# Storing the last output piece by two DMAs from two queues

## The chip, the cores and the metric

The kernel runs on one core of a Trainium2 chip. The metric is the device time of one execution in microseconds; medians of repeated runs are quoted, with the lowest and highest. *Span* is the time from the first to the last instruction in the profile; it is listed for every run, to 0.1 us, so that a single difference of time and span is good to 0.05 us. *Tail* is the part of the span after the end of the last VectorE addition, read from the profiled run. Times finer than the printed lines (1617.775 where a line has 1617.78), first packets of single DMAs and landings come from the records of the same trace.

## The reference

Four blocks with residual connections on x of 2048 tokens by 1024 columns, in bf16: linear attention, gated feed-forward, and the same two again. Only the end of the last block matters here:

```python
def _B_ref(x, w_gate, w_up, w_down):
    g = jnp.einsum("bsd,df->bsf", x, w_gate)
    u = jnp.einsum("bsd,df->bsf", x, w_up)
    h = g * u
    return jnp.einsum("bsf,fd->bsd", h, w_down)
...
x = x + _B_ref(_layernorm(x, axis=-1), B_w_gate, B_w_up, B_w_down)
return x
```

## The kernel before

X holds all tokens in 16 tiles of 128 tokens. In the last block each tile's sum is added to X by VectorE and stored at once by SyncE. The last tile is done in three column pieces of 512, 384 and 128 columns, so that little is left to add and store after the last matmul:

```python
def add_store(t, a, b, ps, last):
    nc.vector.tensor_tensor(out=X[:, t, a:b], in0=X[:, t, a:b], in1=ps, op=ALU.add)
    if last:
        nc.sync.dma_start(out=o_view[:, t, a:b], in_=X[:, t, a:b])
...
def d_end(t):
    def run():
        tl = t % TPG
        for a, b in ((0, 512), (512, 896), (896, 1024)):
            ps = mm_tile()
            for f in range(KF):
                nc.tensor.matmul(out=ps[:, 0, 0:b - a], lhsT=hT[:, f, tl * P:(tl + 1) * P], rhs=wd[f][:, a:b],
                                 start=(f == 0), stop=(f == KF - 1))
            add_store(t, a, b, ps[:, 0, 0:b - a], True)
    return run
```

All DMAs of the program are issued by SyncE. At the end SyncE waits for the semaphores of all of them, two in each wait instruction, and then all engines meet in a barrier.

## Time and profile before

| | before |
|---|---|
| time, 3 runs | 1622.09 us (1621.53 to 1622.28) |
| span of the profiled run | 1620.06 us |
| TensorE busy | 1607.5 us |
| last VectorE addition ends | 1617.75 us |
| last store: start, first packet, last packet, landing | 1617.78, 1618.60, 1618.88, 1619.23 us |
| tail | 2.31 us |

The change can act only on the last row, the tail. The lines behind the table stand in the prediction.

### The profile page before, as it was taken

To read this page: it belongs to the slowest core of one execution; us is meant where nothing else is said; L and a number is where in the kernel's file an instruction comes from. 1 tells how busy PE (TensorE), PEld (TensorE's weight loads), DVE (VectorE), ACT (ScalarE), POOL (GpSimd) and SP (SyncE) were. 2 spreads that over 40 slices of the span, in tenths; PEclk is the share of its full clock that TensorE was granted. 3 is DMA by queue.
4 is the path that set the end of the run, shared out by engine and by line. 5 is a ranking of instruction groups with operands and counts; after the bars stand their busy time and mean duration, and the time that the engine had idled before them with its cause. 6 is when DMAs were issued, how large, how long until landed. Compare 5 with 4: busy or idle time off the path is not lost.

```text
span 1620.1 us, 18047 instructions
## 1 busy us (share of the span) xinstructions
PE 1607.5 (99%) x7710; PEld 734.5 (45%) x7861; DVE 616.6 (38%) x946; ACT 284.0 (18%) x384; POOL 54.5 (3%) x135
## 2 busy tenths in 40 slices
PE   9999999999999999999999999999999999999999
PEld 4444444444444444444444444444444444444444
DVE  6899853202311321243255798432123113211111
ACT  5522201101110110011045231011011101101110
POOL 2100000000000000010000000000000000000000
DMA  8224856512650552142420257655236306521400
GB/s 247 53 72 93 246 162 176 162 52 60 171 159 0 147 162 81 52 156 66 92 52 1 78 114 219 181 157 165 69 102 175 127 20 173 165 66 65 156 1 26
DMA packets 236719, 183.10 MB, mean 113 GB/s; under 512 B 102368, under 2 KB 217312, under 8 KB 236640
## 3 DMA queue, kind: packets, MB, share of 16 engines
q1 hardware_dynamic: 236640, 181.95, 39.0%
q8 instruction: 61, 1.00, 0.3%
q14 instruction: 18, 0.15, 0.0%
HBM read 153.09 MB, written 4.19 MB: 97 GB/s over the span
## 4 chain that ended last, share of the span: by engine, by line
PE 99%; issue 1%; DMA 0%; SPq 0%; DVE 0%
PE ps L196 50%; PE ps L538 48%; PE ps L565 1%; DMA W<-in_A_wqkv_dram 0%; PE kv L306 0%; SPq L109 0%; PE pm L328 0%; PE ps L328 0%; DVE X L546 0%
## 5 line engine op out<-in xcount | busy, mean ns | idle before, releaser
L538 PE MATMUL ps<-xT,R 128*128 128x512 bf16 x2382 | 525.9, 379 | 2.6
L538 PEld LDWEIGHTS <-R 128*128 128x128 bf16 x2432 | 238.0, 98 | 286.9
L542 DVE TENSOR_TENSOR R<-gs,ps 128x512 bf16<-128x512 f32 x224 | 153.9, 687 | 533.5 <-ACT gs L541 533.5
L196 PEld LDWEIGHTS <-R 128*128 128x128 bf16 x2248 | 220.0, 98 | 265.2
L541 ACT COPY gs<-ps 128x512 f32<-128x512 f32 x224 | 131.3, 586 | 1040.2 <-PE ps L538 1011.5
L538 PE MATMUL ps<-xT,W 128*128 128x512 bf16 x1130 | 250.4, 379 | 1.2
L196 PEld LDWEIGHTS <-xT 128*128 128x128 bf16 x1536 | 149.5, 98 | 181.4 <-issue 1.9
L196 PE MATMUL ps<-W,xT 128*128 128x512 bf16 x997 | 222.8, 379 | 1.9 <-issue 0.3
L538 PEld LDWEIGHTS <-W 128*128 128x128 bf16 x1152 | 112.7, 98 | 135.9
L196 PE MATMUL ps<-W,R 128*128 128x512 bf16 x733 | 170.1, 379 | 0.8
L546 DVE TENSOR_TENSOR X<-X,ps 128x1024 bf16<-128x1024 bf16 (+3 forms) x34 | 39.4, 1158 | 335.8 <-PE ps L196 282.8
L196 PE MATMUL ps<-R,R 128*128 128x512 bf16 x506 | 111.8, 379 | 0.4
L196 PE MATMUL ps<-PQ,R 128*128 128x512 bf16 x488 | 111.4, 379 | 0.5
L196 PE MATMUL ps<-R,xT 128*128 128x512 bf16 x502 | 110.3, 379 | 0.5
L201 ACT ACTIVATE e<-ps 128x1024 bf16<-128x1024 f32 x56 | 57.3, 1024 | 141.2 <-PE ps L196 86.0
L175 DVE BATCH_NORM_STATS2 st<-X 128x6 f32<-128x512 bf16 x128 | 81.7, 680 | 0.1
L179 POOL TENSOR_SCALAR ve<-mv 128x1 f32<-128x1 f32 x64 | 16.2, 254 | 1325.8 <-DVE mv L177 1325.8
L196 PE MATMUL ps<-GL,R 128*128 128x512 bf16 x240 | 57.8, 379 | 0.3
L196 PE MATMUL ps<-xT,R 128*128 128x512 bf16 x240 | 57.5, 379 | 0.2
L378 DVE TENSOR_TENSOR X<-X,ps 128x1024 bf16<-128x1024 bf16 x32 | 38.7, 1209 | 17.0 <-PE ps L196 17.0
L186 DVE TENSOR_SCALAR R<-X,mv,rstd 128x1024 bf16<-128x1024 bf16 x64 | 33.7, 542 | 27.3 <-POOL rstd L181 24.0
L205 DVE TENSOR_SCALAR e<-e 128x1024 bf16<-128x1024 bf16 x64 | 26.9, 421 | 38.1 <-ACT e L201 38.1
(73 smaller groups left out, 456.6 us busy)
## 6 DMA issues: line engine op xcount, KB each, us to landing
R<-in_B_w_gate_dram SPq DMA_DIRECT2D x38, 1024.0 KB, 5.4
R<-in_B_w_up_dram SPq DMA_DIRECT2D x38, 1024.0 KB, 7.6
W<-in_B_w_gate_dram SPq DMA_DIRECT2D x18, 1024.0 KB, 5.4
W<-in_B_w_up_dram SPq DMA_DIRECT2D x18, 1024.0 KB, 7.6
W<-in_A_wqkv_dram SPq DMA_DIRECT2D x10, 1024.0 KB, 6.2
W<-in_B_w_down_dram SPq DMA_DIRECT2D x6, 1024.0 KB, 11.2
X<-in_A_x_dram SPq DMA_DIRECT2D x16, 256.0 KB, 6.7
PQ<-in_B_w_down_dram SPq DMA_DIRECT2D x4, 1024.0 KB, 8.4
```

The costliest lines, as they stand in the source:

```text
L175: nc.vector.bn_stats(out=st[:, c, :], in_=X[:, t, c * NB:(c + 1) * NB])
L179: nc.gpsimd.tensor_scalar(out=ve[:], in0=mv[:, 1:2], scalar1=1e-5, scalar2=None, op0=ALU.add)
L186: nc.vector.tensor_scalar(out=dst, in0=X[:, t, :], scalar1=mv[:, 0:1], scalar2=rstd[:], op0=ALU.subtract, op1=ALU.mult)
L196: nc.tensor.matmul(out=ps[:, n, :], lhsT=lhsT, rhs=rhs[:, n * NB:(n + 1) * NB], start=start, stop=stop)
L201: nc.scalar.activation(out=e[:], in_=flat(ps), func=ACT.Exp, **sc)
L205: nc.vector.tensor_scalar(out=e[:], in0=e[:], scalar1=1.0, scalar2=EPS, op0=ALU.min, op1=ALU.add)
L378: nc.vector.tensor_tensor(out=X[:, t, :], in0=X[:, t, :], in1=flat(ps), op=ALU.add)
L538: nc.tensor.matmul(out=ps[:, n, :], lhsT=w[:, k, j * P:(j + 1) * P], rhs=xT[g % 2][:, k, :], start=(k == 0), stop=(k == KD - 1))
L541: nc.scalar.copy(out=gs[:], in_=ps[:, 0, :])
L542: nc.vector.tensor_tensor(out=hT[:, f, :], in0=gs[:], in1=ps[:, 1, :], op=ALU.mult)
L546: nc.vector.tensor_tensor(out=X[:, t, a:b], in0=X[:, t, a:b], in1=ps, op=ALU.add)
L565: nc.tensor.matmul(out=ps[:, 0, 0:b - a], lhsT=hT[:, f, tl * P:(tl + 1) * P], rhs=wd[f][:, a:b], start=(f == 0), stop=(f == KF - 1))
```

## The change

The intent is to shorten the tail: two queues issue half of the last piece each, so that each DMA has half of the tokens to move.

```diff
-                add_store(t, a, b, ps[:, 0, 0:b - a], True)
+                nc.vector.tensor_tensor(out=X[:, t, a:b], in0=X[:, t, a:b], in1=ps[:, 0, 0:b - a], op=ALU.add)
+                if b < D:
+                    nc.sync.dma_start(out=o_view[:, t, a:b], in_=X[:, t, a:b])
+                else:
+                    for eng, h in ((nc.sync, 0), (nc.scalar, 64)):
+                        eng.dma_start(out=o_view[h:h + 64, t, a:b], in_=X[h:h + 64, t, a:b])
```

## The prediction

> **What bounds the kernel now.** I read the page first, its engine shares and the chain of work that ended last.
>
> ```profile
> PE 1607.5 (99%) x7710; PEld 734.5 (45%) x7861; DVE 616.6 (38%) x946; ACT 284.0 (18%) x384; POOL 54.5 (3%) x135
> ...
> PE 99%; issue 1%; DMA 0%; SPq 0%; DVE 0%
> PE ps L196 50%; PE ps L538 48%; PE ps L565 1%; DMA W<-in_A_wqkv_dram 0%; PE kv L306 0%; SPq L109 0%; PE pm L328 0%; PE ps L328 0%; DVE X L546 0%
> ```
>
> TensorE is busy for 1607.5 of 1620.1 us and the chain is 99% matmuls. The change touches no matmul. It can act only on what follows the last matmul, so I went to the end of the span: the chain and the timeline of the last microseconds.
>
> ```profile
> 1609.85 7.58 PE ps L565 x62
> 1617.44 0.02 issue
> 1617.46 0.29 DVE X L546
> ...
> 1616.48 1.63 SPq L548 DMA_DIRECT2D out_dram<-X  x2
> ...
> 1617.46 0.29 DVE L546 TENSOR_TENSOR X<-X,ps 128x128 bf16<-128x128 bf16 x1 [1.01 <-PE ps L565]
> ```
>
> The columns are start, duration, what. The last matmul group ends at 1617.44. VectorE adds the last 128 columns until 1617.75. The printed chain stops there, because it ends with the last compute instruction; the span goes on to 1620.06, so the tail is 2.3 us. The DMA view of the window from 1617.77 to 1620.1 us, in 40 slices of 58 ns, holds the last store alone, and the waits of SyncE's queue say what the end waits for.
>
> ```profile
> DMA  0000000000000028841000000000000000000000
> ...
> q1 hardware_dynamic: 144, 0.03, 6.4%
> ...
> out_dram<-X SPq DMA_DIRECT2D x1, 32.0 KB, 1.5
> ...
> SPq L648 <- DMA out_dram<-X: 0.9, 1, 0.9
> L648 SPq DRAIN  x3: 7/7/7, 1619.3 to 1619.6; - x3
> ```
>
> The store is released at 1617.78 (unrounded start 1617.775, from the trace's records, as are the finer times below). Its issue instruction lasts 332 ns. Its packets move only from 1618.60 to 1618.88, slices 15 to 19 of the 40. It lands at 1619.23, that is 1.45 us after its start. SyncE stands 0.9 us in its final semaphore waits for that landing. The closing barrier of all engines then takes until 1620.06. So the tail is 0.03 of release, 0.83 from issue to first packet, 0.27 of movement, 0.35 from the last packet to the landing, and 0.83 for SyncE's last waits and the barrier. Only the 0.27 depends on how many rows and bytes this DMA holds; the rest is the same whatever the size. The four stores of the last token tile show that.
>
> ```profile
> out_dram<-X SPq DMA_DIRECT2D x1, 256.0 KB, 2.0
> out_dram<-X SPq DMA_DIRECT2D x1, 128.0 KB, 1.7
> out_dram<-X SPq DMA_DIRECT2D x1, 96.0 KB, 1.6
> out_dram<-X SPq DMA_DIRECT2D x1, 32.0 KB, 1.5
> ```
>
> Eight times the bytes cost only 0.55 us more (2.001 against 1.451), some 2.5 ns per KB. The first packet came 0.83 us after the start in all four.
>
> **What the Trainium skill says.** "DMA: Bandwidth & Descriptors", section "Rules for kernel authors", has this very change: for two transfers to disjoint partition halves it says not to bother, since both halves are spread over all 16 DMA engines and share them. The trace before has no split store; it fits in that the 128-row store made 144 packets: 128 of data and 16 small ones that signal, one for each engine. The section "Issuing engines are not separate DMA queues" of the same page adds that issuing from several engines saves only the sequencer's issue time. Here that time isn't repeated (one DMA, 332 ns), so there is none to save. Its section "Why a DMA increments its semaphore by 16 and not by 1" gives the number of engines used as the largest number up to 16 that divides the outer dimension: 64 rows still use 16, four rows on each instead of eight. "Perfetto Trace Analysis", section "DMA Instruction — HWDGE (DVE, Sync)", says that one descriptor generator is locked for one issuer at a time, and that the signal follows only after the write is confirmed. The 0.35 us between last packet and landing agrees with the second. Nothing in this trace tests the first, as only SyncE issues DMAs in it.
>
> **The change part by part.** I compared the built programs engine by engine. TensorE, VectorE and GpSimd have the same instructions in the same order (15,724 rows on TensorE). SyncE's last store becomes 64x128 instead of 128x128. ScalarE, idle since its last copy at 1569.6, gets one semaphore wait and one DMA issue, released by the same VectorE addition as SyncE's. So up to 1617.75 nothing moves.
>
> *Removed:* half of the last SyncE store. From 2.5 ns per KB, 16 KB less is 0.04 us. As a bound from the other side, half of its 0.27 us of movement is 0.14 us. But the other half of the rows goes through the same 16 engines at the same moment, so on each engine eight rows are still to be moved. I take 0.05 us as the most that SyncE's half gains.
>
> *Added:* one DMA on a queue that this program has never used. Its fixed path is 0.83 + 0.35 us, beside SyncE's, not after it, if the two issue in parallel. I count 16 more signalling packets as nothing. Three costs could push it out:
> (a) If the descriptor generator serves one issuer at a time, ScalarE's issue starts up to 0.33 us after SyncE's.
> (b) The first DMA of a queue may be slower: SyncE's own first, at 0.723 us, put its first packet 1.035 us after its start against 0.83 in the stores, 0.2 us more. It is a load while the stores are not, so this is a weak estimate.
> (c) ScalarE's issue instruction may last longer than 332 ns; no record here.
>
> *Moved:* the two completion semaphores. Before, the last store signals on the semaphore that SyncE's fifth and last final wait looks at. In the built program afterwards ScalarE's half has that place and SyncE's half signals on one that the third wait looks at. Those waits stand 64 ns apart in the trace (1618.153, 1618.217, 1618.279, 1618.343). If SyncE's half lands at 1619.18, waits three to five end no earlier than 0.13 us after that, some 0.08 us later than today. So even with perfectly parallel halves the end gains nothing: minus 0.05, plus 0.13.
>
> *Sum:* with a small lag of ScalarE's half, the end moves by +0.05 to +0.1 us. With (b) alone, +0.15. With (a) in full, +0.28 (0.33 less 0.05). With (a) and (b), about +0.5. I choose +0.2, a little under half of the worst, since (a) is stated by a page and its size isn't. 1622.09 + 0.2 = 1622.3 us.
>
> **The rivals.** *1. The split shortens the tail.* For it: the engines are idle in this window (6.4% of it) and each DMA has half of the rows. Against it: 0.27 us is all there is to halve, both halves use the same engines, and the wait order gives 0.13 us back. At best minus 0.1 us: 1622.0. *2. Issue on ScalarE is serialised or cold, and its landing becomes the bound.* For it: the locked generator of the page, and 0.2 us for SyncE's first DMA. Against it: 332 ns may be mostly the sequencer's own work; an issue with eight times the descriptors (a weight load, 128x8x512) takes 368 ns at the median, so the generator need not be held for all of it. 1622.4 to 1622.6. *3. A second queue costs something outside the span,* such as setting it up or clearing it at each launch. The time is 1.74 us above the span of the profiled execution (1621.84 against 1620.1), so such work would hide there. Nothing in the trace speaks for it; it could add some tenths of a microsecond.
>
> **The range and the chances.** The mechanism spans minus 0.1 to plus 0.5 us, against three runs of before from 1621.53 to 1622.28, a spread of 0.75 us. The run-to-run spread is larger than the effect, so it makes the range: 1621.6 to 1623.0. Two per cent is 32 us; the whole tail is 2.3 us. Only a run in an unusual state could cross it: faster 0.005, within 2% 0.99, slower 0.005.
>
> **What would show it.** In the changed profile the last VectorE addition still ends within some tenths of 1617.75, TensorE's busy time stays at 1607.5, and there are two stores of 16 KB, one from SyncE and one from ScalarE. SyncE's should land in 1.40 to 1.45 us. ScalarE's landing decides the rivals: under 1.5 us after SyncE's start means parallel issue, 1.6 to 1.65 means a cold queue, near 1.75 means a serialised issue. From landing to the span's end should stay near 0.83 us. The prediction is wrong if the span shrinks by more than 0.1 us, if it grows by over 0.5, or if the time moves while the span doesn't, which would be rival 3.

## The result, and the profile after

The changed kernel took 1622.91 us (1622.51 to 1623.15, six runs); the kernel before, in six runs, 1621.95 us (1621.53 to 1622.28). The ratio is 1.0006, with a 95% interval from 0.9993 to 1.0019: the same within 2%. (A ratio is the mean time of one kernel's fast runs over that of the other's of the same rounds, so it is not quite the ratio of the medians.) The six runs of each do not overlap, though: the change costs about 1 us.

The page of the changed kernel: engine shares, the two queues that carry its DMAs, and the chain.

```profile
PE 1607.3 (99%) x7710; PEld 734.7 (45%) x7861; DVE 616.5 (38%) x946; ACT 283.9 (18%) x384; POOL 54.3 (3%) x135
...
q1 hardware_dynamic: 236576, 181.94, 39.1%
...
q10 hardware_dynamic: 80, 0.02, 0.0%
...
PE 99%; issue 1%; DMA 0%; SPq 0%; DVE 0%
```

The body is as before. The new queue, q10, carried 80 packets: 64 rows and 16 signals. The timeline of the end follows (start, duration, engine, what):

```profile
1617.16 0.29 DVE L567 TENSOR_TENSOR X<-X,ps 128x128 bf16<-128x128 bf16 x1 [1.01 <-PE ps L565]
1617.47 0.56 SPq L572 DMA_DIRECT2D out_dram<-X  x1
1617.48 0.57 ACTq L572 DMA_DIRECT2D out_dram<-X  x1
```

Both issues start within 5 ns of each other, 0.03 us after the addition, but last 555 and 573 ns, where the one store before lasted 332. The DMA view of the window from 1617.47 to 1620.36 us, in 40 slices of 72 ns, then the wait of SyncE's queue for the landings, and SyncE's last drains:

```profile
DMA  0000000000000000143025300000000000000000
...
out_dram<-X SPq DMA_DIRECT2D x1, 16.0 KB, 1.8
out_dram<-X ACTq DMA_DIRECT2D x1, 16.0 KB, 2.0
```

```profile
SPq L653 <- DMA out_dram<-X: 1.3, 2, 1.1
```

```profile
L653 SPq DRAIN  x3: 7/7/7, 1619.6 to 1619.9; - x3
```

SyncE stands 1.3 us in its final waits, where it stood 0.9 us before. There are two bursts of packets, one after the other, and both come late. In times after the addition's end, so that the two kernels can be laid side by side:

| us after the last addition | before | after, SyncE's half | after, ScalarE's half |
|---|---|---|---|
| issue starts | 0.027 | 0.028 | 0.033 |
| first packet | 0.856 | 1.224 | 1.495 |
| last packet ends | 1.128 | 1.451 | 1.719 |
| landed | 1.478 | 1.800 | 2.066 |
| span ends (the tail) | 2.313 | 2.916 | 2.916 |

So the tail grew by 0.60 us: SyncE's half lands 0.32 us later than the whole piece did, ScalarE's half 0.27 us after that, and 0.01 us is in what follows the last landing. The span of the profiled run grew by only 0.30 us, since its last addition ended 0.30 us earlier (1617.45 against 1617.75). I take that for scatter: over the 25 repeated runs of the kernel before that the experiments below brought, the span varies from 1619.6 to 1620.4 us, and the profiled run of the changed kernel is the shortest of its six (1620.4 to 1621.0). The tail, in contrast, repeats to about 0.01 us (2.31, 2.31, 2.31, 2.32 and 2.32 in five profiled kernels whose end is that of before). Two more kernels have the same last store, the two probes, and a tail of 2.39 and 2.38 us: their last store lands as before (1.48 and 1.47 us after the addition), but on a semaphore that an earlier one of SyncE's final waits looks at, and 0.91 us pass from there to the end instead of 0.83 to 0.85.

A second part shows only when time and span are subtracted run by run. In the six runs of the changed kernel the time is 2.07 to 2.15 us above the span; in the kernel before it is 1.74 to 1.83 us above it, in all of those 25 runs. This part, 0.33 us, lies outside the span. Together, 0.60 and 0.33 make 0.93 of the 0.96 us between the medians.

The questions were therefore: why are both halves late, why is ScalarE's later still, and what costs 0.33 us outside the span?

### The profile page after: what moved, and what is told of

The parts are those of the page before. It is cut to its first block, busy times and chain, and to the rows that moved or that the text cites. A ratio compares the mean times of both kernels' runs of the same rounds, so it can differ in the third digit from the quotient of the medians.

```text
span 1620.4 us, 18049 instructions
## 1 busy us (share of the span) xinstructions
PE 1607.3 (99%) x7710; PEld 734.7 (45%) x7861; DVE 616.5 (38%) x946; ACT 283.9 (18%) x384; POOL 54.3 (3%) x135
## 4 chain that ended last, share of the span: by engine, by line
PE 99%; issue 1%; DMA 0%; SPq 0%; DVE 0%
PE ps L196 50%; PE ps L538 48%; PE ps L565 1%; DMA W<-in_A_wqkv_dram 0%; PE kv L306 0%; PE pm L328 0%; PE ps L328 0%; SPq L109 0%; PE pt L403 0%; DVE X L567 0%
## 5 line engine op out<-in xcount | busy, mean ns | idle before, releaser
L546 DVE TENSOR_TENSOR X<-X,ps 128x1024 bf16<-128x1024 bf16 x31 | 37.8, 1221 | 326.1 <-PE ps L196 282.8
L378 DVE TENSOR_TENSOR X<-X,ps 128x1024 bf16<-128x1024 bf16 x32 | 38.7, 1208 | 17.0 <-PE ps L196 17.0
```

The source lines that it names most:

```text
L378: nc.vector.tensor_tensor(out=X[:, t, :], in0=X[:, t, :], in1=flat(ps), op=ALU.add)
```

## The experiments

Every kernel below that was timed in repeated runs is the same as before within 2%, so the comparisons rest on the tail and on time less span. The edits of "Both halves from SyncE", "Two pieces split", "Split by columns" and "96 and 32 tokens" are shown against the changed kernel, those of "The whole piece from ScalarE", "An early store from ScalarE" and the two probes ("Many forms in one run", "Token counts") against the kernel before. The probes' single times, 1622.18 and 1621.70 us, are compared with nothing.

The theories of the longer tail: *contention* (two issues at the same moment hinder each other), *form* (a DMA of 64 tokens is slow in itself), and *cold queue* (ScalarE's queue is slow, or slow at its first use). For the part outside the span: use of a second queue, or something else in the program.

### Both halves from SyncE

```diff
-                    for eng, h in ((nc.sync, 0), (nc.scalar, 64)):
+                    for eng, h in ((nc.sync, 0), (nc.sync, 64)):
```

> Both 64-token halves of the last piece go from SyncE's queue, one after the other. Three theories for the longer tail of the changed kernel (2.92 us from the end of the last VectorE addition to the span's end, against 2.31 before). Contention: two issues at the same moment hinder each other (555 and 573 ns, first packets 1.19 and 1.46 us after the start, against 332 ns and 0.83 us for a store alone). Then here, with no second issuer, each half should issue in about 332 ns and put its first packet 0.83 us after its start; the second starts some 0.4 us after the first; tail 2.7 to 2.85 us. Form: a 64-token store is slow in itself, whoever issues it. Then 555 ns each, tail above 3.1 us. Cold queue or slow ScalarE issue: no ScalarE here, so as under contention. Time outside the span (measured time less span: 1.74 us before, 2.1 us after): if a second queue in use costs it, here it is 1.75 us, as before.

The timeline and the DMA view (window from 1617.79 us to the end, slices of 84 ns):

```profile
1617.80 1.18 SPq L572 DMA_DIRECT2D out_dram<-X  x2
```

```profile
DMA  0000000000000024100000440000000000000000
...
out_dram<-X SPq DMA_DIRECT2D x2, 16.0 KB, 1.8
```

With nobody else issuing, the first half took 549 ns to issue, put its first packet 1.219 us after the addition (1.224 in the changed kernel) and landed at 1.793 (1.800). The line shows the pair: 1.18 us for two issues. The second issue took 578 ns. So it is the form, and not contention, that delays SyncE's half; my expectation under contention, 332 ns, was wrong by 217. The tail is 3.37 us and the time 1622.79 us (1622.38 to 1623.14) against 1621.64 (1621.42 to 1622.02). Time less span: 1.74 to 1.85 us. The second half landed 0.938 us before the span's end, where it is 0.835 us in the kernel before: its semaphore is in the third of SyncE's final waits, two more follow.

### The whole piece from ScalarE

```diff
-                add_store(t, a, b, ps[:, 0, 0:b - a], True)
+                nc.vector.tensor_tensor(out=X[:, t, a:b], in0=X[:, t, a:b], in1=ps[:, 0, 0:b - a], op=ALU.add)
+                eng = nc.sync if b < D else nc.scalar
+                eng.dma_start(out=o_view[:, t, a:b], in_=X[:, t, a:b])
```

> The last piece is not split; ScalarE alone stores all 128 tokens of it. Contention: nobody else issues at that moment, so ScalarE's issue takes about 332 to 360 ns, the landing comes about 1.45 us after the start, tail 2.3 to 2.4 us. Cold queue or slow ScalarE issue: about 570 ns and a landing 1.8 to 2.0 us after the start, tail 2.65 to 2.9 us. Form: 128 tokens, so as under contention. Outside the span: 2.1 us if use of ScalarE's queue costs 0.35 us there, so that the time is 0.35 us above before although the tail is the same; 1.75 us if not.

The timeline has the issue, the DMA view the time to landing:

```profile
1618.05 0.38 ACTq L569 DMA_DIRECT2D out_dram<-X  x1
```

```profile
out_dram<-X ACTq DMA_DIRECT2D x1, 32.0 KB, 1.5
```

ScalarE's first and only DMA took 378 ns to issue and landed 1.490 us after its start, 0.04 us later than SyncE's 1.451. The tail is 2.37 us. ScalarE's queue is neither slow nor noticeably cold. The time is nevertheless 1622.33 us (1621.67 to 1622.51), because time less span is 2.09 to 2.17 us; the rest I take for the scatter of the body.

### Two pieces split

```diff
-                if b < D:
+                if a == 512:
                     nc.sync.dma_start(out=o_view[:, t, a:b], in_=X[:, t, a:b])
```

(The 512- and the 128-column pieces are split, the 384-column piece between them is not.)

> The first column piece (512 columns) of the last tile is split over the two queues too, 5.7 us before the last piece, so ScalarE's queue has been used once when the last piece comes. Contention: both pairs look alike, issues of about 555 and 573 ns and first packets 1.19 and 1.46 us after the start; tail about 2.9 us. Cold queue: the first pair is slow, the second issues in 332 ns with a tail of about 2.4 us. Form: both pairs slow. Outside the span: 2.1 us, as in the changed kernel, if it is paid once per launch.

The timeline shows the two pairs, the first and the last piece:

```profile
1612.15 0.55 SPq L572 DMA_DIRECT2D out_dram<-X  x1
1612.15 0.58 ACTq L572 DMA_DIRECT2D out_dram<-X  x1
...
1617.86 0.48 SPq L572 DMA_DIRECT2D out_dram<-X  x1
1617.87 0.51 ACTq L572 DMA_DIRECT2D out_dram<-X  x1
```

The issues of the first pair took 550 and 577 ns, those of the second 476 and 507 ns. ScalarE's half landed 0.26 us after SyncE's in the first pair and 0.27 us in the second. So an earlier use of ScalarE's queue takes nothing off the lag. The second pair's issues are some 70 ns shorter, but on SyncE's queue too, which had been in use all along; a warm queue doesn't explain that. The tail is 2.95 us, against 2.92 in the changed kernel. The time was 1622.56 us (1622.27 to 1623.09). Time less span was 1.76 to 1.82 us, which the expectation had wrong, and which spoke against the second queue as the cause.

### An early store from ScalarE

```diff
-            nc.sync.dma_start(out=o_view[:, t, a:b], in_=X[:, t, a:b])
+            eng = nc.scalar if t == 12 else nc.sync
+            eng.dma_start(out=o_view[:, t, a:b], in_=X[:, t, a:b])
```

> The kernel before, with one change: the whole-tile store of token tile 12, 35 us before the end, is issued by ScalarE instead of SyncE. The tail is untouched and should be 2.31 us. If use of a second queue costs 0.35 us outside the span, the measured time is 0.3 to 0.4 us above before and the difference of time and span is 2.1 us. If that difference in the changed kernel was chance, the time equals before within 0.15 us and the difference is 1.75 us. ScalarE's issue alone: 332 to 360 ns and a landing about 2.0 us after the start by the contention theory, 570 ns or more and 2.2 us or more by the theory of a cold or slow ScalarE queue.

The tail is 2.32 us, as expected, and time less span is 2.07 to 2.11 us; the time was 1622.37 us (1621.80 to 1622.48), of which 0.3 us is that difference; the rest I take for the scatter of the body. ScalarE's issue took 373 ns and landed in 2.05 us; SyncE's stores of that size in the same trace took 1.99 to 2.14, and one 3.14. By itself this would have confirmed the second queue as the cause; the previous run, with two DMAs on that queue and 1.8 us, doesn't fit. What sets the three kernels at 2.1 us apart from those at 1.8 us is the number of instructions in ScalarE's stream of the built program: 694 against 692 or 696. Hence the two kernels with padding below.

### Many forms in one run

The stores of the earlier tiles are 12 us or more apart, so each of them can carry another form. Tiles 0 to 10 and 12 to 14 are cut like this (excerpt; the tail is as before):

```diff
+                0: [(sp, low, full), (sp, high, full)],
+                2: [(sp, (0, 96), full), (sp, (96, P), full)],
+                3: [(sp, (32 * i, 32 * i + 32), full) for i in range(4)],
+                4: [(act, low, full), (act, high, full)],
+                5: [(sp, low, full), (act, high, full)],
+                6: [(sp, whole, left), (act, whole, right)],
```

> The whole-row stores of token tiles 0 to 10 and 12 to 14, each 12 us or more from the next, are cut in different ways, so that one trace measures each form alone; the last tile is stored as before. So far a 64-token store issued alone by SyncE took 549 ns to issue and put its first packet 1.19 us after its start, against 332 ns and 0.83 us for 128 tokens. Form theory: every store of fewer than 128 tokens (32, 64, 96, 112) takes 475 ns or more to issue and about 1.1 to 1.2 us to its first packet, on either queue, whereas stores of all 128 tokens take 332 to 380 ns and 0.83 to 0.9 us, also where only half of the columns go. Rival: 64 tokens in particular are slow, or the second half because it starts at token 64. On ScalarE's lag of 0.27 us in the changed kernel: if the generator serves one store after the other, then two 64-token stores by ScalarE alone put the first packet about 1.25 us after the start, and only where SyncE issues at the same moment is ScalarE's 0.27 us behind it; if ScalarE is just slower with 64 tokens, then 1.46 us alone too. Two 128-token column halves issued at once by both queues: SyncE's as alone, ScalarE's 0.2 to 0.3 us behind if serialised.

A store of 64 tokens that was the first of its tile, with one queue issuing, took 466 to 558 ns to issue and put its first packet 1.12 to 1.21 us after its start, on either queue, from either end of the tile. But 32 tokens took 314 ns and 0.82 us, 96 took 378 and 0.88, 112 took 345 and 0.84. So the rival of the expectation holds: not fewer than 128, but 64 in particular.

ScalarE alone and then both queues at once, with 64 tokens each (timeline and DMA view of tile 4, DMA view of tile 5):

```profile
1292.56 1.20 ACTq L568 DMA_DIRECT2D out_dram<-X  x2
...
out_dram<-X ACTq DMA_DIRECT2D x2, 128.0 KB, 2.4
```

```profile
out_dram<-X SPq DMA_DIRECT2D x1, 128.0 KB, 2.3
out_dram<-X ACTq DMA_DIRECT2D x1, 128.0 KB, 2.6
```

ScalarE alone with 64 tokens: first packet after 1.21 us, landing after 2.33; SyncE alone: 1.20 and 2.31. So ScalarE isn't slower with that form. Where both issued 64 tokens at once, ScalarE's landed 0.31 and 0.34 us after SyncE's; where both issued 128 tokens by 512 columns at once, 0.17 us. The lag in the changed kernel comes from issuing at the same moment, then. It isn't a longer issue: beside SyncE, ScalarE's two took 496 and 504 ns, alone 558 and 473. Its first packet was 0.62 and 0.43 us behind SyncE's, where it is 0.27 us in the changed kernel, whose halves have an eighth of the bytes.

### Split by columns

```diff
-                    for eng, h in ((nc.sync, 0), (nc.scalar, 64)):
-                        eng.dma_start(out=o_view[h:h + 64, t, a:b], in_=X[h:h + 64, t, a:b])
+                    for eng, c in ((nc.sync, a), (nc.scalar, a + 64)):
+                        eng.dma_start(out=o_view[:, t, c:c + 64], in_=X[:, t, c:c + 64])
```

> The last piece is split by columns, not by tokens: 128 tokens x 64 columns on SyncE's queue, 128 tokens x 64 columns on ScalarE's. Form theory: with all 128 tokens in each, both issue in 332 to 380 ns; SyncE's lands about 1.45 us after its start, ScalarE's 0.05 us later if parallel, 0.3 us later if serialised by one generator; tail 2.4 to 2.65 us, so shorter than the changed kernel's 2.92 and not shorter than 2.31. Contention theory (already in doubt, since a 64-token store alone was as slow): issues of 550 ns and a tail near 2.9 us. Outside the span: 2.1 us, as its ScalarE stream has as many instructions as the changed kernel's.

The same bytes, two queues at the same moment, but 128 tokens in each. Timeline and DMA view (window from 1617.75 us to the end, slices of 61 ns):

```profile
1617.76 0.33 SPq L572 DMA_DIRECT2D out_dram<-X  x1
1617.76 0.37 ACTq L572 DMA_DIRECT2D out_dram<-X  x1
```

```profile
DMA  0000000000000069951000000000000000000000
...
out_dram<-X SPq DMA_DIRECT2D x1, 16.0 KB, 1.4
out_dram<-X ACTq DMA_DIRECT2D x1, 16.0 KB, 1.6
```

Both issues are back at 332 and 373 ns, and the packets form one burst instead of two. SyncE's half landed 1.444 us after the addition, 0.03 us before the whole piece of the kernel before: that is all that half of the bytes gains here. ScalarE's landed at 1.608. The tail is 2.46 us: 0.46 us shorter than with the split by tokens, 0.15 us longer than with no split. The time is 1622.52 us (1622.32 to 1622.61) against 1621.89 (1621.40 to 1622.23), with 2.07 to 2.13 us outside the span.

### 96 and 32 tokens

```diff
-                    for eng, h in ((nc.sync, 0), (nc.scalar, 64)):
-                        eng.dma_start(out=o_view[h:h + 64, t, a:b], in_=X[h:h + 64, t, a:b])
+                    for eng, h, n in ((nc.sync, 0, 96), (nc.scalar, 96, 32)):
+                        eng.dma_start(out=o_view[h:h + n, t, a:b], in_=X[h:h + n, t, a:b])
```

> The last piece is still split by tokens over the two queues, but 96 tokens to SyncE and 32 to ScalarE. The theory now: a store of 64 tokens in particular is slow to its first packet (1.12 to 1.21 us in ten stores of the run with mixed forms, against 0.82 for 32, 0.88 for 96, 0.83 for 128), and it holds back a store issued by the other queue at the same moment by 0.27 us, one of 128 tokens by 0.12 us. Then here SyncE's issue is under 400 ns with its first packet near 0.88 us, ScalarE's is about 0.1 us later, and the tail is 2.4 to 2.5 us. Rival: any split by tokens is slow at the tail; then 2.8 to 2.9 us. Outside the span 2.1 us, ScalarE's stream having 694 instructions.

The issues in the timeline, then size and time to landing in the DMA view:

```profile
1617.89 0.35 SPq L572 DMA_DIRECT2D out_dram<-X  x1
1617.90 0.41 ACTq L572 DMA_DIRECT2D out_dram<-X  x1
```

```profile
out_dram<-X SPq DMA_DIRECT2D x1, 24.0 KB, 1.5
out_dram<-X ACTq DMA_DIRECT2D x1, 8.0 KB, 1.6
```

The piece is still split by tokens, on the same two queues at the same moment, but no DMA has 64. The issues take 348 and 412 ns, SyncE's part lands 1.480 us after the addition, ScalarE's 0.165 us later, the tail is 2.48 us. This is the changed kernel without its 64; 0.44 of its 0.60 us are gone. The time was 1622.50 us (1622.39 to 1622.81) against 1621.88 (1621.57 to 1622.11), with 2.09 to 2.18 us outside the span.

### Token counts

SyncE alone stores the earlier tiles with a cut at 16, 32, 48, 64, 72, 80, 96 or 112 tokens, and once 64 tokens that begin at token 32:

```diff
+            cuts = {0: (48,), 1: (80,), 2: (16,), 3: (64,), 4: (32,), 5: (96,), 6: (112,), 7: (72,),
+                    8: (32, 96), 9: (48,), 10: (80,), 12: (64,), 13: (32,), 14: (96,)}.get(t, ())
```

> SyncE alone stores tiles in token counts of 16, 32, 48, 64, 72, 80, 96 and 112, the rest of the tile after it, and 64 tokens from token 32 on once. If 64 in particular is slow, 48, 72 and 80 issue in under 400 ns and put their first packet 0.8 to 0.9 us after the start, and 64 alone stands at 470 to 550 ns and 1.12 to 1.2 us, wherever it begins. If it is a range of counts around 64, then 48 and 80 are slow too.

The timeline of two tiles, cut at 80 and at 64 tokens (two issues in each line, both parts together one tile):

```profile
1159.12 0.79 SPq L555 DMA_DIRECT2D out_dram<-X  x2
1183.29 1.18 SPq L555 DMA_DIRECT2D out_dram<-X  x2
```

| tokens in the first DMA of the tile | issue, ns | first packet after, us |
|---|---|---|
| 16 | 314 | 0.82 |
| 32 | 347, 361 | 0.85, 0.86 |
| 48 | 315, 362 | 0.81, 0.86 |
| 64 | 498, 556; 597 from token 32 | 1.15, 1.20; 1.25 |
| 72 | 358 | 0.78 |
| 80 | 317, 317 | 0.82, 0.81 |
| 96 | 317, 317 | 0.82, 0.82 |
| 112 | 316 | 0.82 |

Among the first DMAs of a tile, only 64 stands out. It isn't confined to that DMA, though: where the 64 tokens began at token 32, the 32 tokens issued right after them took 575 ns to issue, whereas 32 tokens after a first part of 96 took 425 and 426. Why the number 64 does, these runs don't tell; nothing in the trace shows what happens between an issue and its first packet.

### ScalarE's stream two instructions longer, without and with the change

In both kernels, before and after, two tiny ScalarE copies are added at the start, where ScalarE waits for its first data:

```diff
     nc.scalar.activation(out=warm[:], in_=mhalf[:], func=ACT.Exp)
+    for _ in range(2):
+        nc.scalar.copy(out=warm[:], in_=mhalf[:])
```

> The kernel before with two more tiny ScalarE copies at the start, while ScalarE waits for its first data; ScalarE issues no DMA. So far the difference of measured time and span was 1.8 us where ScalarE's stream has 692 instructions (before; both halves on SyncE) or 696 (two split pieces), and 2.1 us in all three kernels where it has 694. Theory: it is the length of ScalarE's instruction stream, not the use of its DMA queue. Then here, with 694, the difference is 2.1 us and the time about 0.3 us above before with a tail of 2.31 us. Rival: one DMA on ScalarE's queue costs it (and two do not, which is odd). Then 1.75 to 1.8 us and the time of before.

> The changed kernel with the same two tiny ScalarE copies: 696 instructions on ScalarE, one DMA on its queue. Length theory: the difference of time and span goes back to 1.8 us, the tail stays 2.9 us, and the time is about 0.6 us above before instead of 0.95. Queue theory: the difference stays at 2.1 us.

The kernel before, padded to 694 instructions, has the tail of before (2.31 us), no DMA on ScalarE's queue, and 2.08 to 2.15 us outside the span; its time is 1622.20 us (1621.94 to 1622.85) against 1621.89. The changed kernel, padded to 696, keeps its tail (2.91 us) and its DMA on that queue and has 1.73 to 1.83 us outside the span; its time is 1622.43 us (1622.11 to 1622.98), 0.54 us above before instead of 0.96. So the cost outside the span doesn't come from the queue. Nor does it follow the length of the other streams: both halves on SyncE and the probes lengthen SyncE's and stay at 1.8 us, and the whole piece from ScalarE shortens it by two and has 2.1 us.

### One and three instructions more

The same edit to the kernel before with `range(1)` and `range(3)`.

> The kernel before with one tiny ScalarE copy more at its start, 693 instructions in ScalarE's stream. With 692, 696 and 708 the time stood 1.8 us above the span, with 694 it was 2.1 us, whatever the DMAs. If only streams whose length is a multiple of four cost 1.8, this one shows 2.1 us; if only the odd pairs (694) are dear, 1.8 us. Tail 2.31 us either way.

> The same with three tiny ScalarE copies more, 695 instructions. Multiple-of-four theory: 2.1 us above the span. Otherwise 1.8 us. Tail 2.31 us either way.

Neither rule of the expectations holds. With 693 instructions the time is 1.84 to 1.89 us above the span, with 695 it is 1.90 to 1.95; the tails are 2.31 and 2.32 us, the times 1621.71 (1621.47 to 1621.99) and 1622.04 us (1621.64 to 1622.30) against 1621.88. Put in order: 692, 696 and 708 instructions about 1.8 us, 693 1.87, 695 1.93, 694 2.1. With the unrounded spans of the profiled runs they are 1.78 to 1.81, 1.83, 1.94, and 2.11 to 2.15; so 693 is hardly above the first group. The three multiples of four agree, but each other remainder was seen at one length only: whether it is a pattern in the remainder isn't shown. What produces the difference lies outside the profiled span and stays open.

No version came out that beats the kernel before: every split left a second DMA that lands after the first, and halving the bytes gains 0.03 us.

## Why the prediction was right or wrong

**The outcome.** 1622.91 us lies in the range, near its upper end, and the class is the one given 0.99. The argument for the narrow class, that the change touches only the tail of 2.3 us, held but for the 0.33 us outside the span. The place in the range is luck in part: I chose +0.2 us, the mechanism's worst case was +0.5, and 0.96 was measured; the allowance for scatter between runs took it in. The prediction's own signs say so: SyncE's half landed 1.77 us after its start instead of 1.40 to 1.45, ScalarE's 2.04 us after SyncE's start, later than the 1.75 that was to mean a fully serialised issue. The tail grew by more than the 0.5 us at which the prediction was to be wrong; the span of the profiled run, by which that was put, grew by only 0.30, because the body of that run, the shortest of the six, happened to be shorter.

**Nothing moves before the last addition.** Right. TensorE is busy for 1607.3 us against 1607.5, and the addition ends within 0.3 us of its old place.

**Removed: SyncE's half gains at most 0.05 us.** This is the step that failed. It took the 0.83 us from issue to first packet as the same for any size, because four stores of 256 to 32 KB had shown that. (Three of them are the last tile's; the one of 256 KB is the whole tile before it.) All four had 128 tokens: I had varied the bytes per token and not the number of tokens. With 64 tokens it is 1.20 us; the half lands 0.32 us later instead of 0.05 earlier. The gain itself was about right: the packets of the 64 tokens moved in 0.23 us instead of 0.27, and with the split by columns the half landed 0.03 us earlier.

**Added, (a), a serialised issue, up to 0.33 us.** Right that issuing at once costs the second DMA time: 0.27 us in the changed kernel (ScalarE alone isn't late). Not shown is that the issue is serialised: both start within 5 ns and last 555 and 573 ns, and the lag appears as a later first packet. It is about 0.165 us where neither DMA has 64 tokens, so half of what I had allowed for. Whether the generator or the 16 engines make ScalarE wait is argued on either side by these numbers and settled by none.

**Added, (b), a cold queue, 0.2 us.** Wrong: ScalarE's first DMA landed 0.04 us later than SyncE's, and the pair that came after a first use of the queue kept its lag. **(c)**, a longer issue on ScalarE: 0.04 us.

**Moved: the wait order, 0.13 us.** The built program was read rightly, but the cost didn't arise here, since ScalarE's half, on the last wait, lands 0.27 us after SyncE's. It shows where the semaphore of the third wait comes last: both halves on SyncE, and two split pieces, had 0.94 us from the last landing to the end. Against 0.83 to 0.85 where it is the fifth wait's, that is about 0.1 us; in the probes, where it is the fourth's, it was 0.91.

**The sum.** In place of +0.2 us: 0.32 (form, less the gain of half the bytes) + 0.27 (issued at once) + 0.01 after the landing = 0.60 in the tail, and 0.33 outside the span.

**The rivals.** The first, a shorter tail, is out, and with it the idea of the change. The second, ScalarE's landing as the bound, is what happened, though SyncE's late half is the greater part of it. The third, a cost outside the span, was right that there is one and wrong about its cause: it follows the length of ScalarE's instruction stream, which the change made longer by two.

## What to carry to other kernels

At the end of a kernel count a store by its fixed path, not by its bytes: here 1.18 of 1.45 us didn't depend on the size, so halving it gained 0.03 us at most, while a second DMA issued at the same moment lands 0.16 us or more after the first. If a store has to be cut, look at the issue time of that very form in a trace; cutting by columns or at 96 tokens issued as a whole store does, cutting at 64 did not. When a change of a microsecond is at stake, compare the tail and the time outside the span each by itself, since the body's scatter is as large as the effect.

## What the Trainium skill lacked or had wrong

- "DMA: Bandwidth & Descriptors", section "Rules for kernel authors": its advice against transfers to two disjoint partition halves held (+0.60 us in the tail), but the reason it gives, the shared 16 engines, misses the greater part. Neither that page nor another that I read says that a DMA of 64 partitions is slow by itself: 466 to 597 ns to issue and 1.12 to 1.25 us to its first packet as the first of its tile issued by one queue, against 314 to 378 ns and 0.78 to 0.88 us for 16, 32, 48, 72, 80, 96 and 112.
- "Perfetto Trace Analysis", section "DMA Instruction — HWDGE (DVE, Sync)": a generator locked for one issuer would let one be expected to wait for the other. Two 128-token stores issued at once both issue in the time of a store alone (332 and 373 ns), and the second's first packet is 0.08 us behind; with 64 tokens it is 0.27 us behind. Sizes of this are lacking.
- "Runtime: NRT & Kernel Launch", section "The ~15µs preamble/postamble breakdown": it lists the stages around a kernel, and nothing in it tells that time outside the span varies with the length of an engine's instruction stream: 1.8 us with 692, 696 or 708 ScalarE instructions in the built program, 1.87 with 693, 1.93 with 695, 2.1 with 694.
